# A 32x128 matrix in place of an FFN whose signs are proven constant, with the old kernel behind a branch

## The chip, the cores and the metric

One NeuronCore of a Trainium2 chip runs one program. The metric is the device time of that core in microseconds. Its engines are PE (matrix products), DVE (vector work), ACT (activation functions and copies), POOL (further element-wise work) and SP, whose queue issues most DMAs.

## The reference

```python
B, N, m, C = (4, 12480, 32, 128)      # x: B x N x C (0.1 randn), inducing: m x C (0.331 randn)
scale = 1.0 / np.sqrt(C)

def mab(q, kv):
    s = scale * (q @ kv.transpose(0, 2, 1))
    s = s - s.max(-1, keepdims=True)
    a = np.exp(s)
    a /= a.sum(-1, keepdims=True) + 1e-09
    return a @ kv

h = mab(I, x)                         # 32 rows per batch, I is inducing for each batch
x2 = mab(x, h).reshape(B * N, C)      # 49920 tokens
hid = x2 @ w_in                       # w_in: 128 x 2048, float64
out = np.maximum(0.01 * hid, hid) @ w_out     # w_out: 2048 x 128, float64
```

Each token's attention result is a mixture of 32 rows of `h` with positive weights. Its hidden values are therefore the same mixture of 32 rows of `h @ w_in`, one number for each of the 2048 FFN units.

## The kernel before

The tokens of a batch lie in six groups of 2048 (32 tokens x 16 x 4) and a rest of 192. For each batch the kernel first makes `h`: x is transposed, the first scores against `indT` go to a 128x512 bank, a running maximum is kept, the Exp of the scores is transposed on DVE (`ay`), and `value_products` sums 32x128 products. Then `expand_weights` forms `h @ w_in` and repeats its high and low halves over the partitions (`hws`). The second scores give softmax weights per token, which are normalised and transposed, split into a high and a low half and stacked by DMA into `A4` (`stack`, L676).

The FFN then runs in 98 tiles of mostly 512 tokens with 16 slots each, 1568 slots in all. A slot makes 128 hidden units (`ffn_product`, L730), a relu in a rounded form on ACT (`ffn_high`, L743), the remainder on DVE (`ffn_low`, L751), and three products into the tile's output (`second_product`, L769): high by high, low by high, high by low weights. The linear part of the leaky function, 0.01 of everything, is a separate small product at a tile's end (L788). The lines are these:

```python
nc.tensor.matmul(
    ph[:, o : o + w],
    hw[b][1][:, f * P : (f + 1) * P],
    woven(A4[t][:, o : o + w], t), start=True, stop=True)
...
second_product(u, w_hi, live[u][0])
second_product(u, w_hi, live[u][1])
second_product(u, w_lo, live[u][0])
```

Work for the next batch is woven between the slots: generators for scores, values and second softmax advance as the loop over slots goes on. The first batch's opening is an order written out by hand (`ORDER`): loads, transposes `T` (L922) with copies on ACT or DVE (L932), scores `S` (L264), maxima `M` (L955) and `X` (L981), Exps `E` (L1008), transposes `Y` (L1016), values `H` (L1043), and the conversion of the float64 weights (L1092 to L1118). ACT loads a table once, at L932. x is read twice, once as rows and once as blocks for the transposes on DVE.

## Time and profile before

| what | value |
|---|---|
| median of 3 runs | 1486.99 us (1486.62 to 1487.38) |
| span of the profiled execution, first to last instruction | 1484.9 us |
| PE, DVE, ACT, POOL busy | 1477.2, 1256.8, 999.8, 112.4 us |
| DMA, mean over the span | 71 GB/s, 105.23 MB |
| read from and written to DRAM | 48.94 and 25.56 MB |

The span is the time of one profiled execution from its first to its last instruction; the runs' median is 2.1 us longer, which is what lies around the span. A matmul's busy time overlaps that of the next one, so PE's work is better read from the starts of its instructions than from their lengths.

### The profile page before, as it was taken

What the parts mean: (1) busy time and instruction counts of PE and PEld (TensorE: products, weight loads), DVE (VectorE), ACT (ScalarE), POOL (GpSimd) and SP (SyncE); (2) the same over time, 40 slices, a digit from 0 to 9 for tenths busy, and PEclk for the clock granted to TensorE, in tenths of its full rate; (3) what the DMA queues carried; (4) which work ended last, traced back from release to release, by engine and by line L of the source; (5) the groups of instructions that cost most, each with busy time, mean ns of one, the idle gap of its engine ahead of it and who ended that gap; (6) DMA issues with size and microseconds to landing.
All of it is one profiled execution on the core that took longest, in us unless ns stands there. A gap on an engine that the chain in (4) does not pass through costs nothing.

```text
span 1484.9 us, 22235 instructions
## 1 busy us (share of the span) xinstructions
PE 1477.2 (99%) x7865; PEld 1263.2 (85%) x7865; DVE 1256.8 (85%) x2115; ACT 999.8 (67%) x1748; POOL 112.4 (8%) x165
## 2 busy tenths in 40 slices
PE   8999999999999999999999999999999999999999
PEld 6788788888789888888878888888888898888887
DVE  6889899779888997879988998888888888888887
ACT  5766676656677766757657676666767766666665
POOL 1320110000000001000001000000101000000000
PEclk9999999999999999999999999999999999999999
DMA  8437344344436325234343531422221212212211
GB/s 287 84 81 135 60 78 78 95 91 81 77 60 132 56 40 137 37 69 90 52 86 86 93 65 33 120 44 49 44 43 29 46 24 49 43 24 47 41 27 22
DMA packets 400255, 105.23 MB, mean 71 GB/s; under 512 B 370544, under 2 KB 373264, under 8 KB 400144
## 3 DMA queue, kind: packets, MB, share of 16 engines
q1 hardware_dynamic: 399952, 103.67, 34.3%
q8 instruction: 62, 1.02, 0.3%
q14 instruction: 49, 0.40, 0.1%
q10 hardware_dynamic: 192, 0.15, 0.0%
HBM read 48.94 MB, written 25.56 MB: 50 GB/s over the span
## 4 chain that ended last, share of the span: by engine, by line
PE 98%; DMA 1%; SPq 0%; issue 0%; ACT 0%; DVE 0%; DVEq 0%
PE po L769 68%; PE ph L730 23%; PE s_ps L264 3%; PE po L788 1%; DMA xr<-in_x_dram 1%; PE h_ps L444 1%; PE h_ps L1043 0%; SPq L894 0%; PE hw_ps L561 0%; PE w_ps L1143 0%; PE winT_ps L1133 0%; PE xT_ps L922 0%; PE last_ps L811 0%; PE a_ps L1224 0%; PE hT_ps L518 0%
## 5 line engine op out<-in xcount | busy, mean ns | idle before, releaser
L743 ACT ACTIVATE ghi<-ph 128x512 fp32r<-128x512 f32 (+1 forms) x1568 | 928.8, 595 | 455.9 <-PE ph L730 449.1
L751 DVE SCALAR_TENSOR_TENSOR glo<-ph,ghi 128x512 fp32r<-128x512 f32 (+1 forms) x1568 | 1040.6, 679 | 195.0 <-ACT ghi L743 170.9
L730 PE MATMUL ph<-A,hws 128*128 128x512 f32 (+1 forms) x1600 | 594.8, 377 | 0.3 <-ACT A L1228 0.3
L769 PE MATMUL po<-glo,w_hi 128*128 128x512 f32 (+1 forms) x1568 | 593.6, 379 | 0.0
L769 PE MATMUL po<-ghi,w_lo 128*128 128x512 f32 (+1 forms) x1568 | 593.5, 379 | 0.0
L769 PE MATMUL po<-ghi,w_hi 128*128 128x512 f32 (+1 forms) x1568 | 593.3, 379 | 0.0
L730 PEld LDWEIGHTS ph<-A,hws 128*128 128x128 f32 x1600 | 302.3, 189 | 55.0 <-DVE e L282 5.0
L769 PEld LDWEIGHTS po<-glo,w_hi 128*128 128x128 f32 x1568 | 296.9, 189 | 40.7
L769 PEld LDWEIGHTS po<-ghi,w_lo 128*128 128x128 f32 x1568 | 296.9, 189 | 40.7
L769 PEld LDWEIGHTS po<-ghi,w_hi 128*128 128x128 f32 x1568 | 297.0, 189 | 39.6 <-ACT ghi L743 0.2
L828 DVE STREAM_TRANSPOSE osb<-po 128x512 f32<-128x512 f32 (+1 forms) x97 | 68.2, 703 | 0.0
L662 POOL TENSOR_TENSOR alo<-aT,ahi 128x512 fp32r<-128x512 f32 x22 | 28.2, 1282 | 473.5 <-ACT ahi L657 407.3
L399 DVE STREAM_TRANSPOSE xT<-xc 128x512 f32<-128x512 f32 x72 | 50.5, 701 | 0.0
L626 POOL TENSOR_TENSOR y<-y,sm 128x512 f32<-128x512 f32 x23 | 24.2, 1050 | 249.9 <-DVE sm L624 235.7
L611 POOL TENSOR_TENSOR y<-y,mx 128x512 f32<-128x512 f32 x23 | 24.2, 1050 | 229.6 <-DVE mx L609 175.4
L788 PE MATMUL po<-A,m2s 128*128 128x512 f32 (+1 forms) x100 | 37.1, 375 | 0.0
L264 PE MATMUL s_ps<-xT,hT 128*32 128x512 f32 x192 | 22.7, 596 | 0.4 <-ACT hT L1087 0.4
L264 PE MATMUL s_ps<-xT,indT 128*32 128x512 f32 x192 | 22.9, 595 | 0.0
L788 PEld LDWEIGHTS po<-A,m2s 128*128 128x128 f32 x100 | 18.9, 189 | 2.5
L359 DVE STREAM_TRANSPOSE y<-s_ps 128x512 f32<-128x512 f32 x22 | 15.6, 716 | 3.1 <-PE s_ps L264 1.4
L444 PEld LDWEIGHTS h_ps<-xr,ay 128*32 128x32 f32 x576 | 15.4, 110 | 2.0 <-issue 2.0
L444 PE MATMUL h_ps<-xr,ay 128*32 128x128 f32 x576 | 17.0, 274 | 0.0
(171 smaller groups left out, 364.0 us busy)
## 6 DMA issues: line engine op xcount, KB each, us to landing
xr<-in_x_dram SPq DMA_DIRECT2D x96, 256.0 KB, 4.4
out_dram<-osb SPq DMA_DIRECT2D x380, 64.0 KB, 2.2
xc<-in_x_dram SPq DMA_DIRECT2D x288, 64.0 KB, 2.7
A<-ahi SPq DMA_DIRECT2D x188, 64.0 KB, 2.0
A<-alo SPq DMA_DIRECT2D x188, 64.0 KB, 2.0
hws<-hilo SPq DMA_DIRECT2D x64, 64.0 KB, 2.0
raw<-in_moe_w_in_dram SPq DMA_DIRECT2D x4, 512.0 KB, 7.0
raw<-in_moe_w_out_dram SPq DMA_DIRECT2D x4, 512.0 KB, 10.0
```

The lines of the kernel that those rows point to most:

```text
L264: nc.tensor.matmul(dst, lhsT, rhs, start=True, stop=True)
L399: nc.vector.transpose(t[:, j, :], blk.rearrange("p n c -> p (n c)"))
L444: nc.tensor.matmul(hp[32 * k : 32 * k + 32, :C], ay[:rows, 4 * q + k, :], xb[:rows, k, :], start=(i == 0 and q == 0), stop=(last[k] == i a ...
L611: engines[0].tensor_tensor(out=yv, in0=yv, in1=mx[:rows, :K].unsqueeze(2).broadcast_to([rows, K, M]), op=ALU.subtract,)
L626: engines[1].tensor_tensor(out=yv, in0=yv, in1=smv.unsqueeze(2).broadcast_to([rows, K, M]), op=ALU.mult)
L662: (engine or nc.gpsimd).tensor_tensor(out=alo[sl], in0=aT.pop((b, g))[: 32 * J, :], in1=ahi[sl].bitcast(F32), op=ALU.subtract,)
L730: nc.tensor.matmul(ph[:, o : o + w], hw[b][1][:, f * P : (f + 1) * P], woven(A4[t][:, o : o + w], t), start=True, stop=True,)
L743: nc.scalar.activation(halves(ghi[:, :n], t)[1], live[u][2], AF.Relu)
L751: nc.vector.scalar_tensor_tensor(out=halves(glo[:, :n], t)[1], in0=ph, scalar=0.0, in1=halves(ghi[:, :n], t)[1].bitcast(F32), op0=ALU.max, ...
L769: nc.tensor.matmul(accs[t][:, :n], w[:, f, :], woven(r[:, :n], t), start=(f == 0 and w is w_hi and r is live[u][0]), stop=False,)
L788: nc.tensor.matmul(accs[t][:, o : o + w], hw[b][2], woven(a4[:, o : o + w], t), start=False, stop=(o + w == n),)
L828: nc.vector.transpose(osb[:, :n], po[:, :n])
```

## The change

The old function stays whole under the name `any_sign_path`. Ahead of it runs a new one, `fixed_sign_path`, which writes the whole output. It makes `h` as before, but transposes x on PE for all batches and keeps the transposed units in nine buffers, so that x is read once. For a batch it takes `h @ w_in` (`hidden`), and for each of the 2048 units the sum over the 32 rows and the sum of absolute values. The sum's sign sets the unit's slope, 1 or 0.01; the sloped 32x2048 matrix times `w_out` is a 32x128 matrix (`fold`), written twice into blocks with a column of ones for the normaliser (`spread`). The output of a token is its unnormalised weights times that matrix, divided by their sum (`output`).

The second scores are made against `h` less its mean. Each unit's largest absolute score goes over all partitions on Pool (`partition_all_reduce` into `most`), and its negative is the bias of the Exp. In `certain` the largest score of the batch, plus a margin, is the bar: a unit's sign is taken as constant if the absolute value of its sum is larger than the bar times its sum of absolute values. `verdict` compares the count of such units with 8192. If all hold, the flag is 0, and the old function, which stands inside a branch on it, is jumped over.

The order of work is that of the loop over `s` and holds for each engine's queue. A step `s` holds the first scores of unit s-1, the second scores of unit s-8, the transposes of unit s, and the outputs of unit s-9.

```diff
-def induced_attention_then_leaky_ffn(
+def any_sign_path(
...
+    STEPS = [[0, 1], [2, 3], [4, 5, RG]]
+    STEP_OF = {g: (p, i) for p, gs in enumerate(STEPS) for i, g in enumerate(gs)}
...
+    ps_t = ctx.enter_context(tc.tile_pool(name="fps_t", bufs=2, space=bass.MemoryType.PSUM))
+    ps_s = ctx.enter_context(tc.tile_pool(name="fps_s", bufs=1, space=bass.MemoryType.PSUM))
+    ps_h = ctx.enter_context(tc.tile_pool(name="fps_h", bufs=1, space=bass.MemoryType.PSUM))
+    ps_o = ctx.enter_context(tc.tile_pool(name="fps_o", bufs=2, space=bass.MemoryType.PSUM))
...
+    def load(b, g, pieces=1):
+        J, K, rows, w = size(g)
+        if g == RG:
+            t = sb.tile([P, K, C], F32, tag="xrr", name="xrr", bufs=2)
+        else:
+            t = sb.tile([P, K, C], F32, tag="xr", name="xr", bufs=6)
+        src, n = rows_of(b, g), K // pieces
+        for i in range(pieces):
+            nc.sync.dma_start(t[:rows, n * i : n * i + n, :], src[:, n * i : n * i + n, :])
+        xr[b, g] = t
...
+    def turn(b, g, q, copy):
+        J, K, rows, w = size(g)
+        n = min(K, 4)
+        if q == 0:
+            if g == RG:
+                xT[b, g] = sb.tile([P, K, rows], F32, tag="xTr", name="xTr", bufs=3)
+            else:
+                xT[b, g] = sb.tile([P, K, rows], F32, tag="xT", name="xT", bufs=9)
+        pt = turn_ps("xT_ps")
+        for k in range(n):
+            nc.tensor.transpose(
+                pt[:, k * rows : (k + 1) * rows], xr[b, g][:rows, 4 * q + k, :], ident[:rows, :rows]
+            )
+        copy(xT[b, g][:, 4 * q : 4 * q + n, :].rearrange("p k t -> p (k t)"), pt[:, : n * rows])
+    def scores(ps, lhsT, b, g):
+        J, K, rows, w = size(g)
+        for j in range(J):
+            nc.tensor.matmul(
+                ps[32 * j : 32 * j + 32, :w].rearrange("p (k r) -> p k r", r=32),
+                lhsT, xT[b, g][:, :, 32 * j : 32 * j + 32], start=True, stop=True,
+                tile_position=(0, 32 * j),
+            )
...
+    def first_scores(b, g):
+        J, K, rows, w = size(g)
+        p, i = STEP_OF[g]
+        if i == 0:
+            rms[b, p] = small("rm", 3)
+        rm = rms[b, p][:, i : i + 1]
+        if J < 4:
+            nc.gpsimd.memset(rm, -3.0e38)
+        sp = score_ps("s1_ps")
+        scores(sp, indT, b, g)
+        e = sb.tile([P, w], F32, tag="er" if g == RG else "e", name="e", bufs=1 if g == RG else 3)
+        nc.vector.tensor_scalar(
+            out=e[:rows], in0=sp[:rows, :w], scalar1=1.0, scalar2=None, op0=ALU.mult, op1=ALU.max,
+            accum_out=rm[:rows],
+        )
+        e_of[b, g] = e
...
+    def maxima(b, p):
+        n = len(STEPS[p])
+        rd = small("rd", 12)
+        nc.vector.tensor_tensor(
+            out=rd[:, : 4 * n].rearrange("p (n j) -> p n j", j=4),
+            in0=rms.pop((b, p))[:, :n].unsqueeze(2).broadcast_to([P, n, 4]),
+            in1=own.unsqueeze(1).broadcast_to([P, n, 4]),
+            op=ALU.mult,
+        )
+        pm = turn_ps("mx_ps")
+        nc.tensor.matmul(pm[:, : 4 * n], same, rd[:, : 4 * n], start=True, stop=True)
+        nm = small("nm", 1, 3)
...
+    def weigh(b, g):
+        J, K, rows, w = size(g)
+        p, i = STEP_OF[g]
+        nm = nms[b, p]
+        if i == 0:
+            zgs[b, p] = small("zg", 3)
+            if p:
+                als[b, p] = small("al", 1, 3)
+                nc.scalar.activation(als[b, p], nms[b, p - 1], AF.Exp, bias=nm, scale=-1.0)
+        zg = zgs[b, p][:, i : i + 1]
+        if J < 4:
+            nc.gpsimd.memset(zg, 0.0)
+        e = e_of.pop((b, g))
+        nc.scalar.activation(
+            e[:rows, :w], e[:rows, :w], AF.Exp, bias=nm[:rows], scale=SCALE, accum_out=zg[:rows]
+        )
+        t = sb.tile([P, K, M], F32, tag="ayr" if g == RG else "ay", name="ay", bufs=1 if g == RG else 4)
+        nc.vector.transpose(t[:rows].rearrange("p k m -> p (k m)"), e[:rows, :w])
+        ay[b, g] = t
...
+    def values(b, g):
+        J, K, rows, w = size(g)
+        p, i = STEP_OF[g]
+        if i == 0:
+            hps[b, p] = value_ps("h_ps")
+        hp, t, rows_in = hps[b, p], ay.pop((b, g)), xr.pop((b, g))
+        last = {q: max(j for j, o in enumerate(STEPS[p]) if q < GROUPS[o][2]) for q in range(4)}
+        for k in range(K):
+            nc.tensor.matmul(
+                hp[32 * (k % 4) : 32 * (k % 4) + 32, :], t[:rows, k, :], rows_in[:rows, k, :],
+                start=(i == 0 and k < 4), stop=(last[k % 4] == i and k + 4 >= K),
+                tile_position=(0, 32 * (k % 4)),
+            )
...
+    def hidden(b):
+        ps = score_ps("H_ps")
+        for c in range(4):
+            nc.tensor.matmul(
+                ps[32 * c : 32 * c + 32, :], hTs[b][:, :M], w_in_sb[:, c].rearrange("p k r -> p (k r)"),
+                start=True, stop=True, tile_position=(0, 32 * c),
+            )
+        HT = sb.tile([P, 16, M], F32, tag="HT", name="HT", bufs=1)
+        nc.vector.transpose(HT.rearrange("p k m -> p (k m)"), ps)
+        sH, aH = small("sH", 16), small("aH", 16)
+        nc.vector.tensor_reduce(out=sH, in_=HT, op=ALU.add, axis=AX.X)
+        nc.vector.tensor_reduce(out=aH, in_=HT, op=ALU.add, axis=AX.X, apply_absolute_value=True)
+        slope = small("slope", 16)
+        nc.vector.tensor_scalar(
+            out=slope, in0=sH, scalar1=0.0, scalar2=SLOPE, op0=ALU.is_gt, op1=ALU.max
+        )
+        sums_of[b] = (sH, aH)
+        G = sb.tile([P, 16, M], F32, tag="G", name="G", bufs=1)
+        nc.gpsimd.tensor_tensor(
+            out=G, in0=HT, in1=slope.unsqueeze(2).broadcast_to([P, 16, M]), op=ALU.mult
+        )
+        return G
+    def fold(b, G):
+        mp = value_ps("m_ps")
+        for k in range(16):
+            nc.tensor.matmul(
+                mp[32 * (k % 4) : 32 * (k % 4) + 32, :], G[:, k, :], w_out_sb[:, k, :],
+                start=(k < 4), stop=(k >= 12), tile_position=(0, 32 * (k % 4)),
+            )
+        mc = small("mc", P, 1)
+        nc.vector.tensor_copy(mc, mp)
+        return mc
+    def spread(b, mc):
+        ms = turn_ps("M_ps")
+        nc.tensor.matmul(ms[:, :P], same, mc, start=True, stop=True)
+        blk = blocks[b % 2]
+        for j in range(4):
+            rows = slice(32 * j, 32 * j + 32)
+            copy = nc.vector.tensor_copy if j % 2 else nc.scalar.copy
+            copy(blk[rows, P * (j % 2) : P * (j % 2) + P], ms[rows, :P])
...
+    def second_scores(b, g):
+        J, K, rows, w = size(g)
+        ps = score_ps("s2_ps")
+        scores(ps, hTs[b][:, M:], b, g)
+        del xT[b, g]
+        peak = small("peak", 1, 3)
+        if J < 4:
+            nc.gpsimd.memset(peak, 0.0)
+        nc.vector.tensor_reduce(
+            out=peak[:rows], in_=ps[:rows, :w], op=ALU.max, axis=AX.X, apply_absolute_value=True
+        )
+        top = most[:, b, g : g + 1]
+        nc.gpsimd.partition_all_reduce(top, peak, P, bass_isa.ReduceOp.max)
+        minus = small("minus", 1, 3)
+        nc.gpsimd.tensor_scalar_mul(minus, top, -1.0)
+        t = sb.tile([P, K, 32], F32, tag="uTr" if g == RG else "uT", name="uT", bufs=2 if g == RG else 3)
+        if J < 4:
+            nc.gpsimd.memset(t[rows:], 0.0)
+        if g == RG:
+            dst, src = t[:rows].rearrange("p k r -> p (k r)"), ps[:rows, :w]
+        else:
+            dst = t.rearrange("p (k a) r -> p a k r", a=4)
+            src = ps.rearrange("p (a k r) -> p a k r", a=4, r=32)
+        nc.scalar.activation(dst, src, AF.Exp, bias=minus[:rows])
+        uT[b, g] = t
+    def output(b, g, kk):
+        J, K, rows, w = size(g)
+        n = min(K // 4, 4) if g != RG else K
+        m = 32 * n
+        if kk == 0:
+            outs[b, g] = sb.tile([P, 4, 4, C], F32, tag="osb", name="osb", bufs=2)
+        osb, t = outs[b, g], uT[b, g]
+        po = ps_o.tile([P, 2, TOK], F32, tag="po", name="po")
+        for h in range(2):
+            part = t[64 * h : 64 * h + 64, n * kk : n * kk + n, :].rearrange("p k r -> p (k r)")
+            nc.tensor.matmul(
+                po[:m, h, : 2 * P + 2], part, blocks[b % 2][64 * h : 64 * h + 64, :],
+                start=True, stop=True, tile_position=(64 * h, 0),
+            )
+        inv = small("inv", 4, 4)
+        inv2 = inv.rearrange("p (h j) -> p h j", h=2)
+        nc.vector.tensor_scalar_add(inv2[:m], po[:m, :, 2 * P :][:, :, :2], 1e-9)
+        nc.vector.reciprocal(inv[:m], inv[:m])
+        nc.vector.tensor_tensor(
+            out=osb[:m, :, kk, :].rearrange("p (h j) c -> p h j c", h=2),
+            in0=po[:m, :, : 2 * P].rearrange("p h (j c) -> p h j c", j=2),
+            in1=inv2[:m].unsqueeze(3).broadcast_to([m, 2, 2, C]),
+            op=ALU.mult,
+        )
...
+    def certain(b):
+        sH, aH = sums_of.pop(b)
+        top, bar, both = small("top"), small("bar"), small("both", 16)
+        nc.vector.tensor_reduce(out=top, in_=most[:, b, :], op=ALU.max, axis=AX.X)
+        nc.vector.tensor_scalar_add(bar, top, MARGIN)
+        nc.vector.scalar_tensor_tensor(
+            out=both, in0=sH, scalar=-1.0, in1=sH, op0=ALU.mult, op1=ALU.max
+        )
+        yes = small("yes", 16)
+        nc.vector.scalar_tensor_tensor(
+            out=yes, in0=aH, scalar=bar, in1=both, op0=ALU.mult, op1=ALU.is_lt
+        )
+        nc.vector.tensor_reduce(out=counts[:, b : b + 1], in_=yes, op=ALU.add, axis=AX.X)
+        low = small("low")
+        nc.vector.tensor_scalar(out=low, in0=top, scalar1=1.0, scalar2=None, op0=ALU.is_lt)
+        nc.vector.tensor_tensor(out=counts[:, b : b + 1], in0=counts[:, b : b + 1], in1=low, op=ALU.mult)
+    def verdict():
+        each = small("each")
+        nc.vector.tensor_reduce(out=each, in_=counts, op=ALU.add, axis=AX.X)
+        ones = small("ones")
+        nc.vector.memset(ones, 1.0)
+        pv = turn_ps("v_ps")
+        nc.tensor.matmul(pv[:1, :1], each, ones, start=True, stop=True)
+        nc.vector.tensor_scalar(
+            out=flag, in0=pv[:1, :1], scalar1=float(B * DFF), scalar2=None, op0=ALU.not_equal
+        )
...
+    NU = B * NG
+    AHEAD = 6
+    setup()
+    load(0, 0, 4)
+    load(0, 1, 4)
+    load_weights(0)
+    load(0, 2)
+    load_weights(1)
+    for g in (3, 4, 5):
+        load(0, g)
+    load(0, RG)
...
+    chain = {}
+    for s in range(NU + 12):
+        if 1 <= s <= NU:
+            b, g = unit(s - 1)
+            first_scores(b, g)
+            if g == NG - 1:
+                first_scores(b, RG)
+        done = []
+        if 2 <= s <= NU + 1:
+            b, g = unit(s - 2)
+            p, i = STEP_OF[g]
+            if g == STEPS[p][1]:
+                done = [(b, p)]
+        for b, p in done:
+            for g in STEPS[p]:
+                values(b, g)
+        if 1 <= s <= NU:
+            b, g = unit(s - 1)
+            p, i = STEP_OF[g]
+            if g == STEPS[p][1]:
+                maxima(b, p)
+                for q in STEPS[p]:
+                    weigh(b, q)
+                total(b, p)
+        for b, p in done:
+            gather(b, p)
+            if p == len(STEPS) - 1:
+                rz = inverse(b)
+                normalise(b, rz)
+        while loaded[0] < NU and loaded[0] <= s + AHEAD and len([k for k in xr if k[1] != RG]) < 6:
+            b, g = unit(loaded[0])
+            load(b, g)
+            if g == NG - 1:
+                load(b, RG)
+            loaded[0] += 1
+        v = s - 8
+        if 0 <= v < NU:
+            second_scores(*unit(v))
+            if unit(v)[1] == NG - 1:
+                second_scores(unit(v)[0], RG)
+        if s >= 7 and (s - 7) % NG == 0 and (s - 7) // NG < B:
+            b = (s - 7) // NG
+            chain["G"] = hidden(b)
+        o = s - 9
+        for q in range(4):
+            if s < NU:
+                turn(*unit(s), q, nc.scalar.copy)
+                if q == 3 and unit(s)[1] == NG - 1:
+                    turn(unit(s)[0], RG, 0, nc.scalar.copy)
+            if q == 0 and "G" in chain and s >= 8 and (s - 8) % NG == 0:
+                b = (s - 8) // NG
+                mc = fold(b, chain.pop("G"))
+                spread(b, mc)
+            if 0 <= o < NU:
+                output(*unit(o), q)
+        if 0 <= o < NU:
+            store(*unit(o))
+            b, g = unit(o)
+            if g == NG - 1:
+                output(b, RG, 0)
+                store(b, RG)
+                certain(b)
+        if converted[0] < 8 and s >= 0:
+            for _ in range(2 if s in (2, 4) else 1):
+                if converted[0] < 8:
+                    convert(converted[0])
+                    converted[0] += 1
+                if weights_loaded[0] < 8:
+                    load_weights(weights_loaded[0])
+                    weights_loaded[0] += 1
+    verdict()
...
+def induced_attention_then_leaky_ffn(tc, x, inducing, w_in, w_out, out):
+    nc = tc.nc
+    with ExitStack() as ctx:
+        keep = ctx.enter_context(tc.tile_pool(name="keep", bufs=1))
+        flag = keep.tile([1, 1], I32, tag="flag", name="flag")
+        with tc.manual_schedule():
+            fixed_sign_path(tc, x, inducing, w_in, w_out, out, flag)
+            undecided = nc.values_load(flag[:1, :1], min_val=0, max_val=1)
+        with tc.If(undecided != 0):
+            any_sign_path(tc, x, inducing, w_in, w_out, out)
...
```

## Rows read from the trace of the kernel before

**Rows 1.** The page's head, busy times, and granted TensorE clock by slice
```profile
span 1484.9 us, 22235 instructions
...
PE 1477.2 (99%) x7865; PEld 1263.2 (85%) x7865; DVE 1256.8 (85%) x2115; ACT 999.8 (67%) x1748; POOL 112.4 (8%) x165
...
PEclk9999999999999999999999999999999999999999
```

**Rows 2.** The page's chain that ended last, by engine and by line
```profile
PE 98%; DMA 1%; SPq 0%; issue 0%; ACT 0%; DVE 0%; DVEq 0%
PE po L769 68%; PE ph L730 23%; PE s_ps L264 3%; PE po L788 1%; DMA xr<-in_x_dram 1%; PE h_ps L444 1%; PE h_ps L1043 0%; SPq L894 0%; PE hw_ps L561 0%; PE w_ps L1143 0%; PE winT_ps L1133 0%; PE xT_ps L922 0%; PE last_ps L811 0%; PE a_ps L1224 0%; PE hT_ps L518 0%
```

**Rows 3.** Groups by line and form: count | busy us, mean ns | idle us, releaser
```profile
L730 PE MATMUL ph<-A,hws 128*128 128x512 f32 x1536 | 583.2, 382 | 0.3 <-ACT A L1228 0.3
L769 PE MATMUL po<-glo,w_hi 128*128 128x512 f32 x1536 | 582.8, 379 | 0.0
```

**Rows 4.** Timeline of the last slots: start us, us, engine, line
```profile
1474.63 0.38 PE L730 MATMUL ph<-A,hws 128*128 128x512 f32 x1
...
1475.49 0.38 PE L730 MATMUL ph<-A,hws 128*128 128x512 f32 x1
```

**Rows 5.** Groups by line and form, the nearest kinds to the new work
```profile
L609 DVE TENSOR_REDUCE mx<-y 128x16 f32<-128x512 f32 x23 | 15.5, 675 | 0.0
...
L922 PE MATMUL xT_ps<-ident,xr 128*128 128x128 f32 x96 | 12.9, 278 | 1.2 <-DMA xr<-in_x_dram 1.2
...
L932 ACT COPY xT<-xT_ps 128x512 f32<-128x512 f32 x15 | 8.4, 586 | 12.1 <-PE xT_ps L922 12.0
...
L1118 POOL TENSOR_TENSOR w_in_sb<-cv_a,cv_t 128x512 int32<-128x512 int32 x4 | 5.5, 1377 | 31.3 <-DVE cv_a L1102 26.3 <-DVE onezg L1006 2.6 <-ACT cv_t L1108 2.4
...
L1118 POOL TENSOR_TENSOR wraw<-cv_a,cv_t 128x512 int32<-128x512 int32 x4 | 5.1, 1277 | 14.4 <-DVE cv_a L1102 5.5 <-PE po L769 4.8 <-PE a_ps L1224 4.1
...
L1008 ACT ACTIVATE e<-e,onenm 128x512 f32<-128x512 f32 x6 | 4.3, 718 | 0.0
L1016 DVE STREAM_TRANSPOSE ay<-e 128x512 f32<-128x512 f32 x6 | 4.2, 702 | 0.0
...
L307 POOL TENSOR_SCALAR four<-rm 32x4 f32<-32x4 f32 x12 | 2.6, 214 | 14.2 <-DVE e L282 13.6
...
L932 ACT ACT_TABLE_LOAD x1 | 1.3, 1283 | 1.2 <-PEq L1405 1.2
...
L1008 ACT ACTIVATION_READ_ACCUMULATOR e<-e,onenm 128x1 f32 x6 | 1.1, 190 | 0.0
...
L1162 DVE TENSOR_TENSOR y<-y_ps,mx 128x512 f32<-128x512 f32 x1 | 0.7, 692 | 0.0
...
L1166 ACT ACTIVATE y<-y 128x512 f32<-128x512 f32 x1 | 0.6, 622 | 0.0
```

**Rows 6.** Timeline of the opening, 12 to 19 us
```profile
13.46 0.08 DVE L955 DVE_READ_ACCUMULATOR e<-s_ps 128x1 f32 x1
...
14.89 2.01 PE L264 MATMUL s_ps<-xT,indT 128*32 128x512 f32 x16
...
16.02 0.69 DVE L955 TENSOR_SCALAR_CACHE_REDUCE e<-s_ps 128x512 f32<-128x512 f32 x1 [0.33 <-PE s_ps L264]
...
17.69 0.17 DVE L974 TENSOR_TENSOR onerd<-onerm,own 128x12 f32<-128x12 f32 x1
...
18.88 0.73 ACT L1008 ACTIVATE e<-e,onenm 128x512 f32<-128x512 f32 x1
```

**Rows 7.** DMA from 10 to 35 us: packets, then issues with us to landing
```profile
DMA packets 5105, 8.52 MB, mean 341 GB/s; under 512 B 408, under 2 KB 2552, under 8 KB 5101
...
raw<-in_moe_w_in_dram SPq DMA_DIRECT2D x4, 512.0 KB, 7.0
raw<-in_moe_w_out_dram SPq DMA_DIRECT2D x4, 512.0 KB, 10.0
```

**Rows 8.** The page's DMA issues, the stores
```profile
out_dram<-osb SPq DMA_DIRECT2D x380, 64.0 KB, 2.2
```

More of the change, by code (lines that the diff above doesn't have):

```diff
@@ L5 @@
 import concourse.tile as tile
-from concourse import mybir
+from concourse import bass_isa, mybir
 from concourse.masks import make_identity
@@ new lines, in induced_attention_then_leaky_ffn @@
+def induced_attention_then_leaky_ffn(tc, x, inducing, w_in, w_out, out):
+    nc = tc.nc
+    with ExitStack() as ctx:
[6 more added lines that the diff above has]
+            any_sign_path(tc, x, inducing, w_in, w_out, out)
```

174 lines of the change are left out of this document (added).

## The prediction

> **What bounds the kernel now.** I read the page first: PE is busy for 1477.2 of 1484.9 us at a granted clock of full speed (9 in every slice, 2.4 GHz), and the others are not near it [rows 1]. Then the chain that ended last: 98% of it is PE, 68% in the second FFN product L769 and 23% in the first L730 [rows 2]. Then the groups by form: 1536 full-width slots, each with one L730 matmul and three of L769 [rows 3]. The timeline of the end shows the beat: one L730 matmul starts at 1474.63 and the next at 1475.49, so a slot costs 0.86 us, and 1568 slots some 1350 us [rows 4]. Last I read the opening of the program, because it does for one batch what the new path does for all four: transposes, scores, maxima, weights, values [rows 5, 6], fed from DRAM at 341 GB/s [rows 7]. These rows price most of the new path.
>
> **Whether the branch is skipped.** The saving exists only if the flag comes out zero, which is a matter of data. Worked out in double precision from the reference's inputs: the largest second score of a batch is 1.42e-4, 1.45e-4, 1.45e-4 and 1.48e-4; with the margin of 1e-5 added, the weakest FFN unit's |sum| over absolute sum is 7.7, 19.1, 10.0 and 29.9 times the bar. Every one of 8192 tests holds, the weakest with a factor of 7.7 to spare, far more than fp32 rounding takes. So the old kernel's instructions are jumped over: all 1350 us of slots, the second load of x, the stacking DMAs, everything.
>
> **What the new path costs, piece by piece.** There are 24 full units (2048 tokens) and 4 rests of 192. A unit moves 1.05 MB in and as much out; with 4.2 MB of weights the path moves 55 MB, at 341 GB/s [rows 7] 162 us. That is a floor, and I find it is not the bound.
>
> A step in the steady part (s = 8 to 24, 17 of them) runs, on PE, the first scores of one unit, the second scores of another, 16 transposes and 8 output matmuls; a group of four score matmuls takes 0.5 us (16 in 2.01), the transposes 0.13 us each (96 in 12.9) [rows 5, 6]. That is some 5 us of PE, less than a third of the step that comes out below. What sets the step is a ring through all engines, because the score bank has one buffer and each engine's work stands in the order of the code: the second scores' Exp waits for Pool's `minus`, and the transposes' copies stand behind that Exp on ACT; the next first scores need the last of these copies. I walk it from Pool's multiply to the next Pool reduce:
> - Exp from the bank 0.62 (nearest row, a 128x512 Exp) [rows 5].
> - Four copies of 0.59 [rows 5]. Two find their transposes ready; the third and fourth wait for 4 x 0.13 us of PE and an output product, since the turn bank has two buffers: 3.2 in all.
> - First scores 0.6, DVE's copy with maximum 0.68 and 0.08 for its accumulator (13.46 on the timeline) [rows 6].
> - Every other step the maxima (17.69 to 18.88 is 1.2 us from `rd` to the first Exp [rows 6]), two Exps of 0.72 with 0.19 each for their accumulators (1.8 together), a DVE transpose of 0.70 [rows 5], all ahead of the peak's reduction on DVE; in the other steps the values and the second scores, 1.5 of PE.
> - The peak's reduction 0.68 [rows 5], and a handover of 0.2 to 0.3 us at each change of engine (0.33 after L264 [rows 6]), five to eight of them.
>
> Summed: about 10.6 with the maxima, 8.3 without, 9.4 as a mean. PE is then idle for most of a step, which it never is in this trace; if its clock fell to 1.2 GHz, the 2.3 us of PE in the ring would double. The bounds are 0 and 2.3; I take 1.2. So 10.6 us.
>
> **The unknown: Pool.** Between peak and Exp stand two Pool instructions: a reduction over all partitions, then a multiplication of 128x1. Pool does no reduction over partitions in this trace. The multiplication is like L307, 0.21 us [rows 5]. For the reduction itself the bounds are that same 0.21 and, from a far row, the longest Pool operation here, 1.38 us [rows 5], run several times over, say 5. I take two of the 1.28 us kind, 2.6: once to exchange and once to spread. The second unknown is larger. An engine that changes to another function may have to load it: ACT does at the start, 1.28 us [rows 5]. Here Pool alternates between two kinds 28 times, so if it holds only one kind's code, it loads 56 times. For one such load the bounds are nothing (the same code stays) and 10.0 us, the slowest fetch from DRAM in the trace; between them are ACT's 1.28 and the 512 KB fetch of 7.0 [rows 7]. What is loaded has to be fetched, and a fetch in one piece is nearest to the 512 KB row, so I take its 7.0. Of the two loads per unit, the one ahead of the reduction starts when the multiplication has ended and is hidden by the 10.6 us of ring; the one between reduction and multiplication has no cover.
>
> The Trainium skill, GPSIMD Engine Reference, section Instruction dispatch, speaks against the change here: Pool's kernels are loadable code, and the first call to a freshly loaded one pays about 6 us without a profiled instruction of its own. No row of this trace shows it, and by its 6 the sum below would be an estimated 570 instead of 610.
>
> **The sum.**
> - Steps 0 to 7: 12.6 MB at 341 GB/s are 37 us; by work, ACT and PE need some 5 us in a step without maxima and 7.4 in one with: 50.
> - 17 steady steps: 10.6 + 2.6 + 7.0 + 0.2 = 20.4 each: 347.
> - 7 steps with second scores alone, and the 4 rests, which pass through Pool behind their batch's last unit: the ring is only Exp, scores and reduction, 2.5 us, so the first load shows too: 7.0 + 2.6 + 7.0 + 0.2 = 16.8 each, 11 of them: 185.
> - Hidden units of a batch (three times in the steady part): Exp, 0.5 of PE, a transpose, two reductions of 0.68 and Pool's product of 1.3 [rows 5] before Pool can go on, mostly beside the ring: 12 together.
> - End: last outputs (four DVE products of 0.69 [rows 5] with their reciprocals), stores landing in 2.2 [rows 8], some ten tiny operations for the verdict, the register load and the jump: 14.
>
> Together 608 us. The median of the runs, 1486.99, is 2.1 over the profiled span of 1484.9; with the same around it: **610 us**. What stands against this in the old kernel is the 1485 us span, all of it.
>
> **The rivals.**
> - *Cheap Pool.* The code stays, and reduction and multiplication cost 0.4 us together. Then a steady step is 11.0, a second-scores step is bound by DVE (0.68 + 4 x 1.0 = 4.7), a rest takes 3.5: 50 + 187 + 33 + 14 + 12 + 14 + 2 = 312 us. For it: no Pool row here shows a load, and all kinds of Pool work in this trace follow each other without gaps of that size beyond their waits. Against it: a new kind of work appears, and ACT's row shows that a new function is loaded. The Trainium skill, same page, section Cross-partition — where GPSIMD wins, gives 247.7 us for a reduction of 128x2048 along the partitions, an estimated 0.12 us for one column; by that alone the reduction would be cheap, and the time near this rival's. Chance 0.08.
> - *Dear Pool.* A load of 10.0 and a reduction of 5: steady steps 10.6 + 5 + 10.2 = 25.8, the other eleven 25.2: 439 + 277 + 78 = 794. This is the upper end of my own case, and with a load of 5.0 and a reduction of 0.2 its lower end: 17 x 16.0 + 11 x 10.4 + 78 = 464. Chance of this whole case 0.87.
> - *The branch is taken.* One test of 8192 failing is enough, at the flag: then the old path runs behind the new one, 610 + 1485 = 2095 us, slower. It is decided where the chip's sum of a unit's 32 values differs from the exact one by over 0.1% of its absolute sum (the bar is 1.5e-4, the weakest unit stands at 7.7 times that), or where the comparison on the chip is not what it seems. For it: the matrix products are fp32 by an engine whose exactness no row shows. Against it: the factor of 7.7. Chance 0.04.
> - *Something in between*, such as loads that are cheap like ACT's 1.28: 312 + 28 x 3.7 = 416. Chance 0.01.
>
> **How the numbers follow.** The likeliest case gives 610. Its bounds are 464 to 794; 450 to 800 leaves out both rivals and the outer cases, somewhat under 2 in 10 with what may exceed my bounds. A measurement of this kernel tells 0.2% (3 us) from no change; nothing but a taken branch or a much dearer Pool comes near that, so faster 0.95, same 0.01, slower 0.04.
>
> **What would show it.** No L730 or L769 work runs; PE is busy for under a third of the span, with granted clock below full speed in the steady part. ACT's wait for `minus` from Pool is the largest wait, about 10 us in each of 28 places; Pool's multiplication starts some 7 us behind its reduction with nothing between. Steps with second scores alone last 17 us, against 20 before them. DMA runs at about 90 GB/s, far from its limit. If the multiplication follows the reduction at once, the cheap rival is right and the largest wait is elsewhere, in the copies behind Exp; if work of the old kernel appears after the verdict, the data rule failed. The forecast is wrong above all if the price of Pool's changes is not 5 to 10 us.

## The result, and the profile after

The changed kernel takes 604.3 us (602.76 to 610.22 in 4 runs) against 1487.0 us of the kernel before on the same chip: a ratio of 0.4071 with a 95% interval of 0.4053 to 0.409. Forecast were 610 us. The profiled execution has a span of 601.0 us and a time of its own of 602.76 us; it is the one read below.

The page after, its head, busy times, and granted TensorE clock by slice, beside [rows 1]:

```profile
span 601.0 us, 5959 instructions
...
PE 289.0 (48%) x2219; PEld 153.3 (26%) x2219; DVE 191.9 (32%) x569; ACT 105.2 (18%) x221; POOL 35.8 (6%) x100
...
PEclk9966957866775596688567558767886565655655
...
issue 62%; PE 17%; DVE 9%; ACT 6%; POOL 4%; DMA 1%; SPq 1%; POOLq 0%; DVEq 0%; ACTq 0%
```

No engine is busy for half of the span. The last line is the chain that ended last: where [rows 2] had 98% PE, it now has 62% "issue", time in which an engine waited for nothing that the profile shows. The clock, 9 in every slice before, is 5 to 9.

The waits of the changed kernel say whose time that is. The columns are us in total, times, longest.

```profile
ACT uT L1735 <- POOL minus L1726: 258.7, 21, 19.6
POOL minus L1726 <- issue: 220.9, 28, 12.0
PEld xT_ps L1541 <- ACT xT L1544: 145.3, 38, 12.8
...
POOL most L1724 <- issue: 29.9, 5, 6.5
```

ACT's Exp waits for Pool's multiplication for 258.7 us, and that multiplication, ready to go as soon as the reduction before it is done, starts 28 times after a gap with nothing in it: 220.9 us, 7.9 us each. The work itself is short, as the groups of Pool show:

```profile
L1724 POOL PARTITION_ALL_REDUCE most<-peak x28 | 10.6, 379 | 265.8 <-DVE peak L1720 128.1
L1726 POOL TENSOR_SCALAR minus<-most 128x1 f32<-128x1 f32 x28 | 7.3, 260 | 220.9 <-issue 220.9
```

What stands at the edge of the gap is seen in the instructions of line 1724 and of line 1726 between 521 and 536 us (durations in ns, then the first and the last start):

```profile
L1724 POOLq MODIFY_POOL_CONFIG  x2: 7/7/7, 522.0 to 522.0; - x2
L1724 POOL PARTITION_ALL_REDUCE most<-peak x1: 376/376/376, 527.8 to 527.8; - x1
...
L1726 POOL TENSOR_SCALAR minus<-most x2: 260/260/260, 521.5 to 535.5; 128x1 f32<-128x1 f32 x2
L1726 POOLq MODIFY_POOL_CONFIG  x2: 83/83/83, 528.1 to 528.1; - x2
```

Pool's sequencer issues two instructions that change Pool's configuration whenever the kind of work changes, at once after the work before: at 522.0, with the reduction 5.8 us behind, and at 528.1, with the multiplication 7.4 us behind. Over the whole run each line has 56 of them, two for each of 28 units. The Trainium skill (GPSIMD Engine Reference, section Instruction dispatch) says that such an instruction can bring in new code and that the first call then pays about 6 us with no instruction of its own to be seen. The gaps ahead of a reduction agree where Pool had to wait for them (5.8 to 6.5 us); those ahead of a multiplication are longer (6.8 to 8.2 us while no x is read), which the Trainium skill does not tell apart. Such a gap is called a load from here on. What it fetches is not to be seen: the queues of instructions in the page's list of DMA queues have 37 packets here, with 57 pairs of configuration instructions, and 35 in the last kernel below, with two pairs.

One steady step in the timeline (start us, us, engine, line), from one multiplication to the next reduction; it is one that also finishes a batch's `h`:

```profile
313.17 0.26 POOL L1726 TENSOR_SCALAR minus<-most 128x1 f32<-128x1 f32 x1 [7.07 <-issue]
313.46 0.69 ACT L1735 ACTIVATE uT<-s_ps,minus 128x512 f32<-128x512 f32 x1 [9.36 <-POOL minus L1726]
...
314.68 1.12 PE L1541 MATMUL xT_ps<-ident,xr 128*128 128x128 f32 x4 [7.17 <-ACT xT L1544]
...
318.04 0.59 ACT L1544 COPY xT<-xT_ps 128x512 f32<-128x512 f32 x1 [1.62 <-PE xT_ps L1541]
319.09 1.70 PE L1549 MATMUL s_ps<-xT,indT 128*32 128x512 f32 x8
...
324.26 1.07 PE L1549 MATMUL s_ps<-xT,hT 128*32 128x512 f32 x8
...
325.39 0.69 DVE L1720 TENSOR_REDUCE peak<-s_ps 128x1 f32<-128x512 f32 x1 [1.61 <-PE s_ps L1549]
...
326.22 0.38 POOL L1724 PARTITION_ALL_REDUCE most<-peak  x1 [12.80 <-DVE peak L1720]
```

The ring is the forecast one: Exp, the copies behind it, first scores, second scores, peak, reduction. It takes 12.8 us here. Windows of the same step (stretch, length, busy us of PE, PEld, DVE, ACT and POOL with counts, then granted clock, DMA share, GB/s) show why PE's part is slow:

```profile
308.00:313.40 5.40, 0.00 (x0) 0.00 (x0) 0.66 (x1) 0.00 (x0) 0.23 (x1) 0.70 0.00 0
314.60:319.00 4.40, 4.32 (x16) 2.44 (x16) 1.03 (x3) 1.69 (x4) 0.00 (x0) 0.50 0.01 4
...
324.20:326.20 2.00, 1.13 (x10) 0.16 (x8) 0.69 (x1) 0.21 (x1) 0.00 (x0) 1.00 1.12 246
```

PE did nothing in the 5.4 us ahead of the multiplication. When it starts again the clock is 0.5, which is 1.2 GHz, and four transposes take 1.12 us and eight score matmuls 1.70; when the clock is back at 2.4 GHz the same eight take 1.07.

At the end the flag is written by 594.8 us, and no instruction of the old kernel's FFN lines is in the trace. The data rule held, and the span ends 6.2 us later.

### The profile page after: what moved, and what is told of

It is laid out like the page before. It is cut to its first block, busy times and chain, and to the rows that moved or that the text cites. A ratio compares the mean times of both kernels' runs of the same rounds, so it can differ in the third digit from the quotient of the medians.

```text
span 601.0 us, 5959 instructions
## 1 busy us (share of the span) xinstructions
PE 289.0 (48%) x2219; PEld 153.3 (26%) x2219; DVE 191.9 (32%) x569; ACT 105.2 (18%) x221; POOL 35.8 (6%) x100
## 4 chain that ended last, share of the span: by engine, by line
issue 62%; PE 17%; DVE 9%; ACT 6%; POOL 4%; DMA 1%; SPq 1%; POOLq 0%; DVEq 0%; ACTq 0%
PE xT_ps L1541 5%; PE po L1748 5%; PE s_ps L1549 4%; ACT xT L1544 2%; PE h_ps L1633 2%; DVE osb L1756 2%; POOL most L1724 2%; ACT e L1606 2%; ACT uT L1735 1%; DVE ay L1610 1%; POOL minus L1726 1%; DMA raw<-in_moe_w_in_dram 1%; PE H_ps L1672 1%; DVE e L1566 1%; DVE peak L1720 1%
## 5 line engine op out<-in xcount | busy, mean ns | idle before, releaser
L1541 PE MATMUL xT_ps<-ident,xr 128*128 128x128 f32 x384 | 84.9, 372 | 127.7 <-ACT xT L1544 127.6
L1748 PE MATMUL po<-blocks,uT 64*128 64x258 f32 (+1 forms) x400 | 96.3, 586 | 25.2 <-DVE inv L1754 21.9
L1541 PEld LDWEIGHTS xT_ps<-ident,xr 128*128 128x128 f32 x384 | 59.0, 189 | 173.1 <-ACT xT L1544 144.9
L1735 ACT ACTIVATE uT<-s_ps,minus 128x512 f32<-128x512 f32 (+1 forms) x28 | 17.7, 634 | 360.2 <-POOL minus L1726 258.7
L1756 DVE TENSOR_TENSOR osb<-po,inv 128x512 f32<-128x512 f32 (+1 forms) x100 | 69.1, 691 | 9.3 <-DMA out_dram<-osb 6.0
L1544 ACT COPY xT<-xT_ps 128x512 f32<-128x512 f32 x96 | 54.0, 586 | 60.5 <-PE xT_ps L1541 60.4
L1748 PEld LDWEIGHTS po<-blocks,uT 64*128 64x128 f32 (+1 forms) x400 | 43.3, 256 | 63.7 <-issue 48.8
L1724 POOL PARTITION_ALL_REDUCE most<-peak x28 | 10.6, 379 | 265.8 <-DVE peak L1720 128.1
L1610 DVE STREAM_TRANSPOSE ay<-e 128x512 f32<-128x512 f32 (+1 forms) x28 | 17.5, 638 | 12.1 <-ACT e L1606 12.1
L1726 POOL TENSOR_SCALAR minus<-most 128x1 f32<-128x1 f32 x28 | 7.3, 260 | 220.9 <-issue 220.9
L1606 ACT ACTIVATE e<-e,nm 128x512 f32<-128x512 f32 (+1 forms) x28 | 18.3, 655 | 11.3 <-DVE nm L1585 11.3
L1755 DVE RECIPROCAL inv<-inv 128x4 f32<-128x4 f32 (+1 forms) x100 | 17.8, 178 | 3.4
```

The source lines that it names most:

```text
L1541: nc.tensor.transpose(pt[:, k * rows : (k + 1) * rows], xr[b, g][:rows, 4 * q + k, :], ident[:rows, :rows])
L1544: copy(xT[b, g][:, 4 * q : 4 * q + n, :].rearrange("p k t -> p (k t)"), pt[:, : n * rows])
L1606: nc.scalar.activation(e[:rows, :w], e[:rows, :w], AF.Exp, bias=nm[:rows], scale=SCALE, accum_out=zg[:rows])
L1610: nc.vector.transpose(t[:rows].rearrange("p k m -> p (k m)"), e[:rows, :w])
L1724: nc.gpsimd.partition_all_reduce(top, peak, P, bass_isa.ReduceOp.max)
L1735: nc.scalar.activation(dst, src, AF.Exp, bias=minus[:rows])
```

## The experiments

The ratios are against the kernel before, with their intervals. The changed kernel's own 604.3 is the point to compare with.

**The multiplication on DVE.** If Pool has no other kind of work between two reductions, nothing is to be loaded there.

```diff
-        nc.gpsimd.tensor_scalar_mul(minus, top, -1.0)
+        nc.vector.tensor_scalar_mul(minus, top, -1.0)
...
-        nc.gpsimd.tensor_tensor(
+        nc.vector.tensor_tensor(
             out=G, in0=HT, in1=slope.unsqueeze(2).broadcast_to([P, 16, M]), op=ALU.mult
```

> The negative of the top score and the hidden units' product move from POOL to DVE, so that POOL has no other kind of work between two reductions over the partitions. Theory (POOL loads code at each change of kind): the 7.9 us mean between the end of a reduction and the negative shrinks to a handover, and the load ahead of the reduction goes as well; 28 x 7.9 = 221 us and some 11 x 5 us for the units that showed the first load: 330 us, 310 to 370. Rival (the reduction itself lasts some 8 us and its record of 0.38 us is only its start): DVE waits just as long for it; only what stood ahead of the reduction can go, 530 to 570 us.

350.5 us, ratio 0.2353 (0.2344 to 0.2362). All of line 1724 in this kernel, and the largest wait of Pool:

```profile
L1724 POOL PARTITION_ALL_REDUCE most<-peak x28: 350/350/380, 80.2 to 330.9; - x28
...
L1724 POOLq MODIFY_POOL_CONFIG  x2: 23/23/23, 57.0 to 57.0; - x2
```
```profile
POOL most L1724 <- DVE peak L1720: 263.7, 28, 23.4
```

The 28 reductions are still there, with two configuration instructions at their line instead of 56, and Pool waits for its data and not for issue. 254 us went with the alternation: the reduction was not the price. Its record is not only its start either: after the reduction at 148.90 us, which ends at 149.25, DVE's multiplication starts at 149.28. (The product `G` moved too, four times 1.05 us.)

One load is new, at the start of the program, ahead of Pool's second instruction for the identity matrix (`masks.py:199`). Its group in this kernel, and under it the same group in the changed one:

```profile
masks.py:199 POOL TENSOR_SCALAR_AFFINE_SELECT ident<-ident 128x128 f32<-128x128 f32 x1 | 0.3, 282 | 9.6 <-issue 9.6
```
```profile
masks.py:199 POOL TENSOR_SCALAR_AFFINE_SELECT ident<-ident 128x128 f32<-128x128 f32 x1 | 0.3, 295 | 0.3 <-POOL ident masks.py:197 0.3
```

In five kernels here Pool's last change of kind is into the reduction (this one and the four without bias), and all five have this gap, 8.8 to 10.2 us; in the other eight traces Pool ends in the other kind, and the same instruction waits at most 0.3. It looks as if Pool starts with the code that the execution before left in it; that was not tried by itself.

**A second multiplication on Pool.** The rival here was that every small Pool instruction has the gap, whatever stood before it.

```diff
-        nc.gpsimd.tensor_scalar_mul(minus, top, -1.0)
+        less = small("less", 1, 3)
+        nc.gpsimd.tensor_scalar_mul(less, top, -0.5)
+        nc.gpsimd.tensor_scalar_mul(minus, less, 2.0)
```

> POOL makes the negative by two multiplications in a row (by -0.5, then by 2). Theory: both need the same code, so the second follows at once, 0.3 us for each of 28 units: 604 + 8 = 612 us. Rival (every small POOL operation pays a wait of some 7 us): 28 x 7.3 = 204 us more, 810 us.

611.3 us, 0.4126 (0.4101 to 0.4151). Pool's timeline:

```profile
218.60 0.38 POOL L1724 PARTITION_ALL_REDUCE most<-peak  x1 [8.37 <-DVE peak L1720]
225.97 0.26 POOL L1727 TENSOR_SCALAR less<-most 128x1 f32<-128x1 f32 x1 [7.00 <-issue]
226.32 0.21 POOL L1728 TENSOR_SCALAR minus<-less 128x1 f32<-128x1 f32 x1
```

The second follows at once, in 0.21 us. The gap belongs to the change of kind.

**One more change and back.** The same, from the other side.

```diff
-        nc.gpsimd.tensor_scalar_mul(minus, top, -1.0)
+        less = small("less", 1, 3)
+        nc.gpsimd.tensor_scalar_mul(less, top, 1.0)
+        again = small("again", 1, 3)
+        nc.gpsimd.partition_all_reduce(again, less, P, bass_isa.ReduceOp.max)
+        nc.gpsimd.tensor_scalar_mul(minus, again, -1.0)
```

> Between reduction and negative POOL makes one more multiplication by 1 and one more reduction over the partitions, so that it changes kind twice more for each unit. Theory: two more loads of some 7.2 us and 0.6 us of work, 28 x 15 = 420 us more, 1025 us. Rival (only the reduction is long): one more reduction of 8 us, 28 x 8 = 224 us more, 830 us.

988.6 us, 0.6647 (0.6623 to 0.6671). Pool's timeline:

```profile
224.76 0.26 POOL L1727 TENSOR_SCALAR less<-most 128x1 f32<-128x1 f32 x1 [7.13 <-issue]
231.15 0.38 POOL L1729 PARTITION_ALL_REDUCE again<-less  x1 [6.13 <-issue]
238.60 0.26 POOL L1730 TENSOR_SCALAR minus<-again 128x1 f32<-128x1 f32 x1 [7.08 <-issue]
```

Two changes more per unit cost (988.6 - 604.3) / 28 = 13.7 us, and the rows say of what: over the run 6.0 us into the reduction and 7.1 into the multiplication, with 0.38 and 0.26 of work. It is 36 us under the forecast: the load into the reduction is the shorter of the two.

**Reads in flight.** In the changed kernel the 28 gaps ahead of the multiplication are 6.8 to 8.2 us where no x is being read when they begin, and 8.6 to 12.0 in the five where it is. That is only a coincidence in time until reads are put where there were none:

```diff
+        if 25 <= s <= 31:
+            for g in range(3):
+                load(0, g)
         v = s - 8
```

> The changed kernel with three further loads of 1 MB of x in each of the seven last steps with second scores, where no load runs otherwise; nothing reads what they bring. There the loads of Pool's code took 6.8 to 7.5 us ahead of the multiplication. If DMA reads in flight lengthen them, the gaps of these steps grow to 8 to 12 us as in the steady part, both of a unit, and the time is 604 + 7 x 2 x 1 to 4 = 620 to 660 us. If the length has nothing to do with reads, the gaps stay at 6.8 to 7.5 and the time at 598 to 611; a store that now lands later behind the loads would show as a wait of VectorE for its output buffer, not in Pool's gaps.

623.0 us, 0.4189 (0.4181 to 0.4198), 19 us more. The windows are five gaps of Pool in these steps, each from the end of one Pool instruction, or up to 0.3 us behind it, to the start of the next (columns as above); the first, third and fifth lie ahead of a reduction, the others ahead of a multiplication:

```profile
518.90:528.10 9.20, 5.37 (x24) 2.05 (x24) 4.54 (x13) 0.41 (x1) 0.00 (x1) 0.69 1.02 363
528.50:538.08 9.58, 0.00 (x0) 0.00 (x0) 0.00 (x0) 0.00 (x0) 0.00 (x1) 0.50 1.01 399
538.40:547.38 8.98, 6.19 (x24) 2.45 (x24) 4.62 (x13) 0.66 (x1) 0.00 (x0) 0.50 0.60 250
547.80:554.70 6.90, 0.00 (x0) 0.00 (x0) 0.00 (x0) 0.00 (x0) 0.00 (x0) 0.50 0.88 203
555.00:563.99 8.99, 6.19 (x24) 2.45 (x24) 4.63 (x13) 0.69 (x1) 0.00 (x0) 0.50 0.72 297
```

When the transfers were issued, the timeline of the same stretch says:

```profile
519.73 4.44 SPq L1495 DMA_DIRECT2D xr<-in_x_dram  x3
526.66 1.79 SPq L1774 DMA_DIRECT2D out_dram<-osb  x4
...
528.49 4.01 SPq L1495 DMA_DIRECT2D xr<-in_x_dram  x3
...
546.90 2.90 SPq L1774 DMA_DIRECT2D out_dram<-osb  x4
...
549.85 2.78 SPq L1495 DMA_DIRECT2D xr<-in_x_dram  x3
```

Reads do lengthen a load: the three into the reduction take 9.0 to 9.5 us by Pool's own rows, where the changed kernel has 5.8 to 6.0 in these steps, and the one into the multiplication that starts together with the reads (528.49) takes 9.6. The fourth gap is the exception that tells more: it starts among stores, the reads are issued 2.1 us into it, and it keeps its 6.9 us. So in these gaps it counts which reads are under way when the load begins, not the traffic over its length; with stores alone the changed kernel's gaps reach 8.2 us. The time came out at the low end of the expectation: of the seven gaps ahead of a multiplication in these steps, only this one grew beyond 8.2 us. What in the chip the two share was not tried.

**The copies ahead of the Exp.** The prediction had the transposes' copies inside the ring, behind the Exp. Here they stand ahead of it, and `hidden` and the rest's second scores move behind the outputs with the Exp; Pool's work is untouched.

```diff
-        nc.scalar.activation(dst, src, AF.Exp, bias=minus[:rows])
         uT[b, g] = t
+        return lambda: nc.scalar.activation(dst, src, AF.Exp, bias=minus[:rows])
...
-            second_scores(*unit(v))
+            weights = second_scores(*unit(v))
...
+        if 0 <= v < NU:
+            weights()
```

> The second scores' Exp moves in ACT's order behind the four copies of the transposes; POOL's two operations are as in the changed kernel. Theory (the copies stand in the ring behind the Exp): the 5.0 us between the Exp's end and the next first scores go in the 16 steady steps, down to the 6.0 us that the load ahead of the reduction takes: 604 - 16 x 4.9 = 525 us, 510 to 560. Rival (the ring is closed by something else, such as the transposes on PE or the stores): over 590 us.

520.6 us, 0.3497 (0.349 to 0.3504). A steady step's Pool rows:

```profile
348.61 0.26 POOL L1726 TENSOR_SCALAR minus<-most 128x1 f32<-128x1 f32 x1 [6.84 <-issue]
355.97 0.38 POOL L1724 PARTITION_ALL_REDUCE most<-peak  x1 [7.09 <-DVE peak L1720]
363.31 0.26 POOL L1726 TENSOR_SCALAR minus<-most 128x1 f32<-128x1 f32 x1 [6.96 <-issue]
```

From multiplication to reduction it is now 7.1 us here, and 8.2 and 9.1 in the steps beside it, where the 14 steady steps of the changed kernel had 12.4 on average: the copies were in the ring. Of the 81 us between the two profiled spans, 68 lie between a multiplication and the next reduction. Another 17 lie in the 28 gaps ahead of the multiplication (203.9 us in all for 220.9), and the start is 4 longer.

**No branch.** The read of the flag, the jump and the old function are left out.

```diff
-            undecided = nc.values_load(flag[:1, :1], min_val=0, max_val=1)
-        with tc.If(undecided != 0):
-            any_sign_path(tc, x, inducing, w_in, w_out, out)
```

> The flag is computed but not read, and the old function with its branch isn't in the program. Theory: reading the flag and the jump cost what lies between the flag's writing at 594.8 and the span's end at 601.0, of which the last stores' landing is a part: 600 us, 596 to 604. Rival (a large program behind a branch costs more, by its instructions' loading or by barriers): under 590 us.

592.1 us (589.8 to 601.6), 0.3981 (0.397 to 0.3993): 12 us less. The trace shows 4.6 of them (the span ends 1.6 us behind the flag instead of 6.2). It is the trace of the slowest run, 601.6 us; the other runs took 589.8 to 593.8, and what the other 7 us are stays open.

**The branch always taken.** The count is compared with 8193.

```diff
-            scalar1=float(B * DFF), scalar2=None, op0=ALU.not_equal
+            scalar1=float(B * DFF + 1), scalar2=None, op0=ALU.not_equal
```

> The flag is compared with 8193, which it can never reach, so the old kernel runs behind the new one in every execution. If the new kernel's 604 us hold none of the old one's work and the two simply follow one another, the time is 604 + 1485 = about 2090 us (2080 to 2110). If part of the old path were already paid for in 604 (its loads, its set-up), it is below 2060; if the old code runs slower behind a branch, above 2130.

2085.2 us in one run. Around the verdict, the timeline:

```profile
595.61 0.15 DVE L1800 TENSOR_SCALAR flag<-v_ps 1x1 int32<-1x1 f32 x1 [0.28 <-PE v_ps L1799]
596.85 0.33 ACTq L137 DMA_DIRECT2D ind<-in_inducing_dram  x1
```

The old kernel's first instruction comes 1.1 us behind the flag, and from there to the end of the 2083.4 us span it takes 1486.6 us, against a span of 1484.9 by itself. In this run the two simply add, so an input that fails one test would pay 40% on top of the old time.

**Without Pool in the steps.** Four kernels ask what bounds the new path once Pool is out of it. They leave out the bias of the Exp: no unit's largest score is taken off; its maxima stay in `most`, and one reduction over partitions per batch, in `certain`, is left of 28. The product `G` is on DVE here too.

```diff
-        nc.gpsimd.partition_all_reduce(top, peak, P, bass_isa.ReduceOp.max)
-        minus = small("minus", 1, 3)
-        nc.gpsimd.tensor_scalar_mul(minus, top, -1.0)
...
-        nc.scalar.activation(dst, src, AF.Exp, bias=minus[:rows])
+        nc.scalar.activation(dst, src, AF.Exp)
```

> The second scores' Exp has no bias, the units' peaks are kept per partition, and POOL reduces over the partitions once per batch, for the test only; the hidden units' product is on DVE. The output divides by the sum, so that the bias changes nothing where the scores are small, and a batch with a top score of 1 or more still goes to the old path. Theory: POOL leaves the ring altogether; the steady step is the ring without POOL, 11 us or less, the steps with second scores alone are bound by DVE at 4.7: 58 + 17 x 10.8 + 7 x 4.7 + 4 x 2.5 + 14 = 298 us, 270 to 320. Rival (something else, such as the transfers or the output products, stands close behind POOL): over 340 us.

337.6 us, 0.2268 (0.2263 to 0.2274), 40 over the forecast. Its steady steps were as forecast (about 10.3 us, without those that hold `hidden`), but the start, up to the first Exp of second scores, took 80 us and not 58. Some 6 of these 22 us are the load ahead of the identity matrix: PE's first transposes start at 10.6 us, and at 4.2 in the changed kernel. The last steps, without transposes, took 4.6 to 11 us where 4.7 were forecast; DVE waited 6.4 us in 6 places for stores to leave the output buffers. So, with a third buffer:

```diff
-        raw = sb.tile([P, TOK, 2], I32, tag="osb", name="raw", bufs=2)
+        raw = sb.tile([P, TOK, 2], I32, tag="osb", name="raw", bufs=3)
...
-            outs[b, g] = sb.tile([P, 4, 4, C], F32, tag="osb", name="osb", bufs=2)
+            outs[b, g] = sb.tile([P, 4, 4, C], F32, tag="osb", name="osb", bufs=3)
```

> The kernel without bias and with one reduction over partitions per batch, with three output buffers in place of two. Theory (its output products wait for the stores of the buffer before, above all in the steps with second scores alone): 338 - 12 = 326 us. Rival (the stores are no bound): 336 to 339 us.

328.0 us, 0.221 (0.2201 to 0.2218), 9.6 us less. DVE's wait for stores is gone, and the last six Exps on full units lie 30.3 us apart instead of 36.1: the stores were a bound at the end. They are not all of it: the weights' `raw` shares these buffers, and the first Exp of second scores starts at 76.3 us instead of 80.0. On this, the copies ahead of the Exp again:

> The same with three output buffers, and the Exp behind the four copies in ACT's order. Theory (the ring of some 10.3 us a step loses the copies and falls to what DVE and PE need, some 8): 326 - 16 x 2.3 = 289 us. Rival (PE or DVE is already the bound of the step): no more than 1% under the kernel with three buffers alone.

327.7 us, 0.2198 (0.2193 to 0.2202): nothing gained, the rival held. What was worth 84 us beside Pool's loads is worth nothing without them. In this kernel PE is 74% busy; that its order of work is the bound was not shown. It waits 20.0 us for DVE, 14.4 at the product of the maxima (`mx_ps`) and 5.6 at the one score bank, some 1.2 us for each of 16 steady steps. The last kernel, on the one with three buffers, was meant to fill that wait; two of the four groups of transposes stand there ahead of the second scores:

```diff
+        if s < NU:
+            for q in range(2):
+                turn(*unit(s), q, nc.scalar.copy)
         v = s - 8
...
-                turn(*unit(s), q, nc.scalar.copy)
+                if q > 1:
+                    turn(*unit(s), q, nc.scalar.copy)
```

> On e7_no_bias_3_buffers, two of the four groups of transposes for the next unit move between the first products and the second scores, so that TensorE has work while it waits for the score bank to be copied out. If that wait (1.2 us in each of 16 steady steps) is TensorE's own lost time, the time falls from 328 to about 309 us. If VectorE or another engine sets the step, or the wait only moves to the next product, it stays at 325 or above.

321.8 us (320.7 to 326.0), 0.2174 (0.2159 to 0.2189): between the two cases. Six of 19 us came. Its waits, and under them two of the same waits in the kernel it is made from:

```profile
ACT uT L1731 <- DVE inv L1750: 26.9, 9, 8.6
PE po L1744 <- DVE inv L1750: 25.3, 35, 2.0
...
ACT uT L1731 <- DVE most L1720: 21.3, 15, 11.0
...
PE mx_ps L1582 <- DVE rd L1575: 13.0, 12, 1.8
```
```profile
ACT uT L1731 <- DVE most L1720: 57.9, 20, 10.1
...
PE mx_ps L1582 <- DVE rd L1575: 13.0, 12, 1.8
```

ACT's wait for the peak fell from 57.9 to 21.3 us, and PE waits 25.3 us for DVE's normalisation of the outputs where it waited 16.1. But most of the wait that was aimed at is untouched: the product of the maxima stands ahead of the moved transposes in PE's queue and waits 13.0 us as before. Only PE's wait at the score bank fell, from 5.9 to 4.0 us. So this edit does not tell what filling the whole wait is worth, and where the six us come from is not shown. This is the fastest version here.

## Why the prediction was right

The mechanism is the forecast one, shown by the first three experiments: Pool changes its kind of work twice per unit, each change costs a load, the one between reduction and multiplication has no cover, and ACT waits for it. That a load brings in code is the prediction's reading; the traces show its price and its configuration instructions, not what is fetched. The branch was skipped. The time came out within 1% partly by luck: 62 us too much for the reduction stood against 25, 25 and 13 too little for the load, the steady ring and the start. The terms in the profiled execution, all 28 units cut at Pool's instructions:

| term | forecast | measured |
|---|---|---|
| up to the first reduction (50, and one ring) | 60.6 | 73.9 |
| reduction, 28 times | 2.6 | 0.38 |
| load ahead of the multiplication, 28 times | 7.0 | 7.89 (6.84 to 11.98) |
| multiplication, 28 times | 0.2 | 0.26 |
| multiplication to next reduction, 14 steady steps | 10.6 | 12.4 (10.5 to 14.5) |
| the same, 9 steps with no ring to cover the load | 7.0 | 6.0 |
| the same, 4 with `hidden` or `fold` between | 47.2 in all | 50.4 in all |
| end | 14 | 10.6 |

Measured, 73.9 + 28 x 8.53 + 173.4 + 53.9 + 50.4 + 10.6 = 601.0; forecast in the same cut, 608. Point by point:

- **The reduction** was mis-sized: 0.38 us for 2.6, 62 us too much in all. The forecast built it from two Pool operations on 128x512 elements; it works on one column. The nearer bound was the small L307 [rows 5].
- **The load** was sized well for a quiet machine and too small under reads of x, +0.9 us on the mean, 25 us in all, some 18 of them in the five gaps that begin behind reads. The prediction took no notice that loads and DMA traffic meet, which the last steps with added reads showed. The other load, ahead of the reduction, takes 5.8 to 6.5 us, and is hidden in the steady steps as forecast: the ring is 12.4 us long.
- **The ring** was 1.8 us short in a steady step. The prediction priced a unit's scores at 0.5 us, from 16 instructions in 2.01 us [rows 6] as four groups of four. A unit takes eight, so that these 16 are two units: the price is 1.0 us, and 1.07 or 1.70 in the step shown, by the clock. For five to eight handovers of 0.2 to 0.3 us the sums hold some 1.0 us, the least of that. The stretch from Exp to first scores is 5.6 us in the step shown, for some 4.2 forecast, at a clock of 1.2 GHz, where 1.2 us were allowed for the clock in the whole ring. That the copies are in it was shown by putting them ahead: some 68 us.
- **The start** is 13 us too short. The first 58 us moved 256 GB/s, not the 341 of [rows 7], at a granted clock of 0.85; which of the two set it was not tried.
- **The last steps** are 13.4 to 14.8 us instead of 16.8, because of the reduction and the load of 6 us.
- **The end** is about as forecast; 4.6 us of it are the flag's way to the jump, shown by leaving it out.

Of the signs named beforehand, three were off: PE is busy for 48% of the span and not under a third, in part because its instructions take longer at the lower clock (a transpose 372 ns on the mean, 278 in [rows 5]) and a unit's scores are eight of them; ACT's wait is 12.3 us (258.7 in 21 places; the other seven the profile puts down to Pool's memsets), not 10; and the last steps are not 17 us. The 93 GB/s and the gap with nothing in it were as told. The cheap rival had one thing right, the reduction itself: the Trainium skill (GPSIMD Engine Reference, section Cross-partition — where GPSIMD wins) led to an estimate of 0.12 us, and the trace has 0.38. It failed at its condition, that the code stays.

## What to carry to other kernels

Count how often an engine changes its kind of work, not only what its instructions cost: two Pool operations of 0.64 us together cost 8.5 us here, and 254 us of 604 went when one of them moved to another engine. Look for such a gap as idle time with "issue" as its releaser and a configuration instruction at its start, also at the start of the program. And judge a reordering only beside the bound that holds at the time: the copies ahead of the Exp gave 84 us beside Pool's loads and nothing without them.

## What the runs showed of the hardware that had not been expected

The two directions of a change of Pool's kind differ: 5.8 to 6.5 us into the reduction, 6.8 to 8.2 into the multiplication, when no read of x is under way at their start. Behind reads they are 8.5 to 9.6 with the reads added, and up to 12.0 in the changed kernel's steady steps. Element-wise products on Pool follow a multiplication without such an instruction, so that they share its kind. Memsets belong to neither: with the multiplication on DVE they stand between reductions (one starts at 132.04 us, the reductions around it at 131.83 and 134.10), and the pair of configuration instructions is not repeated. The five kernels that leave Pool in the reduction's kind have a gap of 8.8 to 10.2 us on Pool at their start, and the other eight traces have none. A branch that skips a whole kernel costs 4.6 us at the end.
